# One Wo pair of the weight stream held in free columns of two PSUM banks and copied to the SBUF ring by VectorE

## Chip, cores and metric

The kernel runs on one core of a Trainium2 chip. The metric is the device time of one execution in microseconds (us). Times of a kernel are given as the median of several runs; the profile is of one further execution.

## What is computed

Two branches share the input x (2048 rows of 640 numbers, bfloat16), and a gate mixes them. Branch A is attention with a small memory that is carried from one segment of 32 rows to the next, 64 segments in all; branch B is a gated feed-forward block. Cut to what matters:

```python
g = sigmoid((x * gate_w).sum(-1, keepdims=True))
for s in range(64):                          # branch A, in order: mem feeds the next segment
    h = concat([mem, xs], axis=1)            # 8 memory rows + 32 rows of x
    q, k, v = h @ Wq, h @ Wk, h @ Wv         # 32 heads of 192
    p = softmax(where(mask, q @ k.T * scale, -1e9))
    o = (p @ v) @ Wo                         # 32*192 -> 640
    mem, out_s = o[:, :8], o[:, 8:]
b = (gelu(x @ w_gate) * (x @ w_up)) @ w_down # branch B
return g * a + (1 - g) * b
```

The memory makes the 64 segments a strict chain: segment s + 1 cannot form Q, K and V before segment s has its output.

## The kernel before

**Three stages.** The kernel first computes branch B and the gates and stores B in HBM. A second stage ("left") forms Q and K for the last 8 rows of x of every segment at once, since these do not depend on the memory; it runs over four octets of heads, uses all eight PSUM banks in turn, and stores the result in HBM. Then come the 64 segments, which take most of the time.

**One segment.** The heads are worked on in four octets. `PROG` (from line 491) is the order of the work inside a segment, written out by hand as a list of steps: ("q", o), ("k", o) and ("v", o) multiply the 32 rows by the weights of octet o (L997 for Q and K, L1025 for V, five pieces of 128 rows of the weight each); ("tq", o) and ("tk", o) transpose the result (L1009); ("sc", o) are the scores (L1071, L1082), ("sm", o) the softmax, ("pt", o) and ("pte", o) the transposed probabilities and their copy to SBUF; ("pv", o) is probabilities times V (L1148, L1150) with the copies out of PSUM by ScalarE (L1158) and VectorE ("uT lo" L1162, "uT hi" L1164). ("wo", o, i) multiplies by two pairs of Wo: `wo_part` takes the 24 pairs in order, four matmuls each (L1177), accumulating in PSUM bank 7. A segment ends with the seam: the result is copied out by VectorE (L1239) and ScalarE (L1241), transposed (L1251 to L1256), and ScalarE writes the new memory rows (L1261), for which the next segment's first Q matmul waits. Vl matmuls (L1036), which prepare V of the left rows for one octet per segment, stand in the seam: up to three pieces ahead of the transposes and the rest behind them.

**The PSUM banks.** Banks 0 to 3 rotate for Q, K, V and the transposes, bank 4 is for Vl, banks 5 and 6 for the scores of even and odd octets and for the transposed probabilities, bank 7 for the Wo sum. A bank has 2 KB per partition. The scores take the first 640 bytes of banks 5 and 6 (4 times 40 float32), the transposed probabilities stay inside those.

**Resident and streamed weights.** The weights of branch A are cut into 84 pieces: 60 of Q, K and V (3,072 bytes per partition, 384 KB) and 24 pairs of Wo (2,560 bytes per partition, 320 KB), 245,760 bytes per partition in all. They do not fit into the 200,128 bytes that SBUF has for them. So a planner, which runs when the kernel is built (from line 541), picks the fewest pieces to stream such that the others fit beside a ring of at least `MINRING` = 18,432 bytes; it picks them at equal steps of estimated time along the segment. The others stay in SBUF from their first load on. The build has 23 streamed pieces, 14 of Q, K and V (q0.3, q1.0, k1.0, k1.3, q2.1, k2.1, k2.3, q3.1, k3.2, v0.0, v0.1, v1.1, v2.1, v3.0, named by octet and piece) and 9 pairs of Wo (1, 2, 5, 9, 11, 14, 17, 21, 23), and a ring of 20,416 bytes.

**The ring.** `ring_load` (L578) takes the next bytes of the ring and has SyncE (SP) issue the load; it wraps at the end. A load waits until the matmuls that read the ring bytes before it are done, so some six or seven pieces are in the ring at once, each at some point between issue and use. SP issues all loads of a segment in one order, the order of use, mixed with the loads of the left rows ("stg", L898), of x, and of branch B's rows, and the stores of the output. `issue_ring` and `piece` (from L587) issue a streamed piece at the latest when the program that is being written out comes to its use; on the chip SP runs ahead of TensorE by as much as the ring allows.

**Waits.** Each tile is a region of SBUF or PSUM (a PSUM bank is one region), and `_Sched` works out from reads and writes what each operation waits for. The engines run their own streams in order.

Of the kernel before, what the change touches and what calls it, by code (L numbers as in the profile page):

```python
# [221 lines left out]
def _build(nc, A_x, A_mem0, A_Wq, A_Wk, A_Wv, A_Wo, seg_len, w_gate, w_up, w_down,  # L222
# [136 lines left out]
    def sreg(o, nbytes, plo=0, phi=128):  # L359
        return Rg("sb", o, o + nbytes, plo, phi)  # L360
# [123 lines left out]
    def piece_size(key):  # L484
        return GO if key[0] == 3 else GQ

    def piece_view(key, o):
        if key[0] == 3:
# [10 lines left out]
    assert NOCT == 4  # L499
    WOP = 6  # L500
    COST = dict(q=0.168, k=0.168, v=0.18, sc=0.6, pt=0.2, pv=0.42, wo=0.285, tq=0.15, tk=0.3)
# [23 lines left out]
    tseg = tt + 0.6  # L525
    npieces = len(order)
    assert npieces == len(set(order)) == 3 * KT * NOCT + NCH // 2
    tot_bytes = sum(piece_size(k) for k in order)
    nstream = 0
    while True:  # L530
        streamed = set()
        for k in range(nstream):
            target = (k + 0.5) * tseg / nstream
            best = min((i for i in range(npieces) if i not in streamed
                        and (order[i][0] == 3 or order[i][2] < (KT - 1 if order[i][0] < 2 else 2))), key=lambda i: abs(tcons[i] - target))
            streamed.add(best)
        if tot_bytes - sum(piece_size(order[i]) for i in streamed) <= res_space - MINRING:
            break
        nstream += 1
    resident_list = [i for i in range(npieces) if i not in streamed]  # L540
    stream_list = [i for i in range(npieces) if i in streamed]
    ring_bytes = res_space - (tot_bytes - sum(piece_size(order[i]) for i in streamed))
    assert ring_bytes <= ffn_base
# [28 lines left out]
    ring_ptr = [0]  # L572
    NSEM = ring_bytes // GO + 2

    def ring_load(key, name):
        n = piece_size(key)
        if ring_ptr[0] + n > ring_bytes:
            ring_ptr[0] = 0  # L578
        o = ring_ptr[0]
        ring_ptr[0] += n  # L580
        reg = sreg(o, n)
        S_.add("sp", lambda e: e.dma_start(piece_view(key, o), piece_src(key)), writes=[reg],
               dma_sem="ring%d" % (stream_counter[0] % NSEM), name=name)
        stream_counter[0] += 1
        return piece_view(key, o), reg
# [3 lines left out]
    def issue_ring(seg, upto):  # L589
        done = issued.get(seg, 0)  # L590
        while done <= upto:
            key = order[stream_list[done]]
            ring_of[(seg, key)] = ring_load(key, "ring s%d p%d" % (seg, done))
            done += 1
        issued[seg] = done

    def piece(seg, key):
        oi = order_index[key]
        assert oi == last_req.get(seg, -1) + 1, "pieces must be consumed in `order`"
        last_req[seg] = oi  # L600
        if seg == 0:
            load_late(oi + LATE)
        if key in res_off:
            assert slot_class[key] != 1 or key in late_in
            return piece_view(key, res_off[key]), r_res[key]
        issue_ring(seg, stream_pos[key])
        return ring_of[(seg, key)]

    late = [key for key in order if slot_class.get(key) == 1]
    late_in = set()  # L610
# [291 lines left out]
    def left_store(o_, s0, s1):  # L902
        st = lst[o_ % 2]
        for lo in range(s0, s1, NSEG // 4):
            hi = lo + NSEG // 4
            S_.add("pool" if o_ == NOCT - 1 else "sp", lambda e, lo=lo, hi=hi: e.dma_start(
                qkl[lo:hi].rearrange("s p c -> p s c")[:, :, 2 * LW * o_:2 * LW * (o_ + 1)],
                st[:, lo:hi].rearrange("p s m c -> p s (m c)")),
                reads=[sreg(ffn_base + o_ % 2 * STB + STB // NSEG * s0, STB // NSEG * (s1 - s0))],
                writes=[Rg("qk", 64 * o_ + lo, 64 * o_ + hi)], dma_sem="lst%d_%d" % (o_ % 2 if o_ < NOCT - 1 else 2, 4 * lo // NSEG),  # L910
                name="left store")

    def first_loads():
        stg_load(0, 0)
        issue_ring(0, 4)

    OB = 7
    nbk = [0]
    for o_ in range(NOCT):
        st, rst_ = lst[o_ % 2], r_lst[o_ % 2]  # L920
        nh = 2 if o_ == NOCT - 1 else 1
        gs2 = [[left_piece((m, o_, k)) for k in range(KT)] for m in range(2)]
        if o_ == NOCT - 1:
            load_late_within(ffn_base, ffn_base + STB)
        for h in range(nh):
            n0, n1, s0, s1 = h * NL // nh, (h + 1) * NL // nh, h * NSEG // nh, (h + 1) * NSEG // nh
            for m in range(2):
                gs = gs2[m]
                for i in range(12):
                    bk = nbk[0] % 8  # L930
                    nbk[0] += 1
                    c = i if m == 0 else kslot(i)
                    S_.add("pe", [lambda e, k=k, g_=gs[k][0], i=i, bk=bk, n0=n0, n1=n1: e.matmul(  # L933
                        ps[:, bk, 0:n1 - n0], g_[:, i * 128:(i + 1) * 128], XL[:, k, n0:n1], start=(k == 0), stop=(k == KT - 1))
                        for k in range(KT)], reads=[x[1] for x in gs] + [r_XL], writes=[r_ps[bk]],
                        name="left o%d m%d c%d" % (o_, m, i))
                    dst = st[:, s0:s1, m, c * M:(c + 1) * M]
                    src = ps[:, bk, 0:n1 - n0].rearrange("p (s i) -> p s i", i=M)
                    rgh = [sreg(ffn_base + o_ % 2 * STB + STB // nh * h, STB // nh)]
                    if i % 2:  # L940
                        S_.add("act", lambda e, dst=dst, src=src: e.activation(out=dst, in_=src, func=ACTF.Copy),
                               reads=[r_ps[bk]], writes=rgh, name="left evac")
                    else:
                        S_.add("dve", lambda e, dst=dst, src=src: e.tensor_copy(out=dst, in_=src),
                               reads=[r_ps[bk]], writes=rgh, name="left evac")
            if h + 1 < nh:
                left_store(o_, s0, s1)
        if o_ == 0:
            mem_init()
            b_load(0)  # L950
            hl_load(4)
            S_.add("dve", lambda e: e.memset(ps[:, OB, :], 0.0), writes=[r_ps[OB]])
        if o_ + 1 < NOCT:
            issue_left(sum(key[1] <= o_ + 1 for key in left_stream) - 1)
        else:
            first_loads()
        left_store(o_, s0, s1)

    S_.add("pool", lambda e: e.memset(pl_sb, 0.0), writes=[r_p])
    S_.add("pool", lambda e: e.memset(Ks[64:128, 8:12, :], 0.0), writes=[r_Kz[0]])  # L960
    S_.add("pool", lambda e: e.memset(Ks[0:64, 12:16, :], 0.0), writes=[r_Kz[1]])
# [64 lines left out]
            ps[32 * j:32 * j + 32, bk, 0:384], lhs, g_[:, 384 * j:384 * (j + 1)],  # L1026
            start=(k == 0), stop=(k == KT - 1), tile_position=(0, 32 * j)) for j in range(4)]

    VB = 4
    vl_left = {}  # L1030

    def vl_mms(s, o, k, g_, rg_):
# [151 lines left out]
    def segment(s):  # L1184
        g, q = s // 4, s % 4
        for item in PROG:
            kind, i = item[0], item[1] if len(item) > 1 else None
            if kind in ("q", "k"):
                m = "qk".index(kind)
                bank = misc_bank()  # L1190
                cmode(s, m, i, bank)
                rows_evac(m, bank)
            elif kind == "stga":
                if s > 0:
                    stg_load(s, 0)
                left_fill(s, 0)
            elif kind == "stgb":
                stg_load(s, 1)
            elif kind == "ost":
                if s > 0:  # L1200
                    out_store(s - 1)
            elif kind == "bld":
                if s > 0:
                    b_load(s)
            elif kind == "hld":
                if s + 1 < NSEG:
                    h_load(s + 1)
            elif kind == "hll":
                if 0 < s < NSEG - 5:
                    hl_load(s + 5)  # L1210
            elif kind == "put":
                if 0 < s < NSEG - 4:
                    hl_put(s + 4)
            elif kind == "mix":
                if s > 0:
                    mix_rows(s - 1)
            elif kind == "tq":
                row_transp(s, 0, i)
            elif kind == "tk":
                row_transp(s, 1, i)  # L1220
            elif kind == "sm":
                probs(s, i)
            elif kind == "sc":
                scores(s, i)
            elif kind == "v":
                v_oct(s, i)
            elif kind == "pt":
                p_transp(s, i)
                if i == 0:
                    p_evac(s, i)  # L1230
            elif kind == "pte":
                p_evac(s, i)
            elif kind == "pv":
                pv_oct(s, i)
            else:
                wo_part(s, item)
# [112 lines left out]
```

## Time and profile before

| | |
|---|---|
| median of 3 runs | 2014.24 us (2010.03 to 2020.6) |
| profiled execution | 2022.26 us, its span in the profile 2020.4 us |
| segments 1 to 62 in the profile | 331.7 to 1991.6 us |

The page of the profile gives busy time, share of the span and number of instructions per engine (PE is TensorE's matmuls, PEld its weight loads, DVE VectorE, ACT ScalarE, POOL GpSimd), then tenths of busy time in 40 equal slices, the DMA queues, and the chain of work that ended last. "Idle before" a group of instructions is named by what ended it. A row of the waits reads: engine and line, what it waited for, us in total, times, longest. A timeline row reads: start, duration, engine, line, operation, how many, and in brackets the idle time before it.

### The profile page before, as it was taken

Reading aid. Unit: us, or ns where it says so; the run is one execution under the profiler, and the core shown is the slowest. Engines: PE = TensorE matmul, PEld = TensorE weight load, DVE = VectorE, ACT = ScalarE, POOL = GpSimd, SP = SyncE. Lnnn points to the kernel's source line nnn. Section 1 sums busy time; section 2 is a strip of 40 time slices with the busy share of each in tenths; the row PEclk is TensorE's granted clock in tenths of the full one; section 3 lists DMA queues with packets and bytes.
Section 4 is the critical chain, followed back from the end, with each engine's and each line's share of the span. In section 5 each row is a group of like instructions: output and inputs, shape, how many; then the busy total and the mean of one; then the engine's idle time right before and its main releaser. Section 6 shows DMA issues by size and latency. Waiting matters only on the chain.

```text
span 2020.4 us, 77475 instructions
## 1 busy us (share of the span) xinstructions
PE 1934.8 (96%) x32897; PEld 1139.4 (56%) x32923; DVE 984.1 (49%) x3215; ACT 846.3 (42%) x2308; POOL 270.8 (13%) x1123
## 2 busy tenths in 40 slices
PE   8999978999999999999999999999999999999999
PEld 4544455555555555555555555555555555555555
DVE  2222324555555555555555555555545555555555
ACT  2222233444444444444444444444444444444444
POOL 2000010111111111111111111111111111111111
PEclk9999989999999999999999999999999999999999
DMA  9706699999999999999999999999999999999998
GB/s 303 213 27 72 183 294 328 332 339 326 327 339 334 323 328 333 335 337 336 340 333 336 331 322 309 335 328 328 330 327 333 327 319 338 336 331 325 330 333 296
DMA packets 399670, 621.18 MB, mean 307 GB/s; under 512 B 91348, under 2 KB 276700, under 8 KB 399324
## 3 DMA queue, kind: packets, MB, share of 16 engines
q1 hardware_dynamic: 387500, 607.82, 90.0%
q10 hardware_dynamic: 10992, 5.27, 1.0%
q8 instruction: 257, 4.21, 0.8%
q0 software_dynamic: 832, 3.15, 0.5%
q14 instruction: 89, 0.73, 0.1%
HBM read 594.99 MB, written 21.11 MB: 305 GB/s over the span
## 4 chain that ended last, share of the span: by engine, by line
PE 76%; DMA 17%; SPq 2%; issue 2%; ACT 2%; POOL 1%; DVE 1%; ACTq 0%; POOLq 0%
PE ps L1177 20%; PE ps L997 18%; DMA arena<-in_A_Wv_dram 9%; PE ps L1025 9%; DMA arena<-in_A_Wo_dram 5%; PE ps L1009 4%; PE ps L933 4%; PE ps L1148 4%; PE ps L834 3%; PE ps L831 3%; PE ps L1082 2%; PE ps L849 2%; PE ps L1036 2%; PE ps L1071 2%; PE ps L1150 1%
## 5 line engine op out<-in xcount | busy, mean ns | idle before, releaser
L997 PE MATMUL ps<-arena 128*32 128x384 bf16 x10240 | 493.5, 328 | 20.0 <-DMA arena<-in_A_Wq_dram 12.1
L1177 PE MATMUL ps<-arena 128*40 128x320 bf16 x6144 | 471.2, 301 | 9.3 <-DMA arena<-in_A_Wo_dram 8.5
L1177 PEld LDWEIGHTS ps<-arena 128*40 128x40 bf16 x6144 | 294.1, 100 | 161.5 <-issue 51.9
L997 PEld LDWEIGHTS ps<-arena 128*32 128x32 bf16 x10240 | 239.7, 96 | 166.3 <-ACT arena L1261 14.1
L1003 ACT ACTIVATE arena<-ps 128x384 bf16<-128x384 f32 x512 | 250.9, 490 | 175.4 <-PE ps L997 170.4
L1025 PE MATMUL ps<-arena 128*32 128x384 bf16 x5120 | 280.3, 329 | 24.1 <-DMA arena<-in_A_Wv_dram 23.3
L964 POOL COPY arena<-arena 128x96 bf16<-128x96 bf16 x256 | 67.2, 263 | 1401.7 <-PE ps L997 325.0
L1158 ACT ACTIVATE arena<-ps 128x320 bf16<-128x320 f32 x256 | 111.6, 436 | 265.4 <-PE ps L1150 265.4
L1060 ACT ACTIVATE arena<-ps 128x384 bf16<-128x384 f32 x256 | 125.5, 490 | 173.4 <-PE ps L1025 172.1
L1025 PEld LDWEIGHTS ps<-arena 128*32 128x32 bf16 x5120 | 125.6, 96 | 124.6 <-DMA arena<-in_A_Wv_dram 50.1
L1093 DVE TENSOR_REDUCE arena<-ps 104x4 f32<-104x160 f32 x256 | 83.2, 325 | 210.7 <-PE ps L1082 210.7
L968 POOL COPY arena<-arena 64x32 bf16<-64x32 bf16 (+1 forms) x768 | 165.3, 215 | 47.3
L1162 DVE CAST arena<-ps 64x160 bf16<-64x160 f32 x256 | 80.4, 314 | 182.1 <-PE ps L1150 181.5
L1009 PE MATMUL ps<-arena 128*128 128x128 bf16 x1536 | 165.6, 222 | 0.7 <-issue 0.7
L1013 DVE COPY arena<-ps 128x384 bf16<-128x384 bf16 x256 | 89.6, 350 | 120.4 <-PE ps L1009 120.4
L1020 ACT ACTIVATE arena<-ps 64x128 bf16<-64x128 bf16 x512 | 137.1, 268 | 6.2
L1009 PEld LDWEIGHTS ps<-arena 128*128 128x128 bf16 x1536 | 87.5, 97 | 75.9 <-issue 21.5
L1148 PE MATMUL ps<-arena 128*128 128x160 bf16 (+1 forms) x768 | 129.0, 258 | 0.0
L1131 DVE TENSOR_TENSOR arena<-ps,arena 128x320 bf16<-128x320 bf16 x256 | 125.3, 489 | 6.0
L1150 PE MATMUL ps<-arena 128*128 128x64 bf16 (+1 forms) x768 | 123.5, 201 | 0.0
L1107 DVE TENSOR_REDUCE arena<-ps 104x4 f32<-104x160 f32 x256 | 81.9, 320 | 62.6 <-ACT ps L1105 59.8
L1105 ACT ACTIVATE ps<-ps 104x160 f32<-104x160 f32 x256 | 72.1, 282 | 94.6 <-DVE ps L1095 93.0
(91 smaller groups left out, 2095.3 us busy)
## 6 DMA issues: line engine op xcount, KB each, us to landing
arena<-in_A_Wo_dram SPq DMA_DIRECT2D x591, 320.0 KB, 5.6
arena<-in_A_Wk_dram SPq DMA_DIRECT2D x336, 384.0 KB, 5.0
arena<-in_A_Wv_dram SPq DMA_DIRECT2D x332, 384.0 KB, 5.7
arena<-in_A_Wq_dram SPq DMA_DIRECT2D x272, 384.0 KB, 5.3
arena<-left_qk_scratch SPq DMA_DIRECT2D x128, 96.0 KB, 5.0
left_qk_scratch<-arena SPq DMA_DIRECT2D x12, 768.0 KB, 8.5
left_qk_scratch<-arena POOLq DMA_DIRECT2D x4, 768.0 KB, 9.3
arena<-in_A_x_dram SPq DMA_DIRECT2D x4, 640.0 KB, 8.7
```

What stands on the lines that cost most here:

```text
L968: S_.add("pool", lambda e, a=a, b=b, lo=lo, hi=hi, sa=sa: e.tensor_copy(out=Ks[lo:hi, a:b, L:R], in_=stg[o // 2][lo:hi, o % 2, 1, sa:sa + ...
L997: S_.add("pe", [lambda e, j=j, k=k, g_=g_: e.matmul(ps[32 * j:32 * j + 32, bank, 0:384], Hb[hb][:, k, 0:L], g_[:, 384 * j:384 * (j + 1)], ...
L1003: S_.add("act", lambda e: e.activation(out=rows_sb[m], in_=ps[:, bank, 0:384], func=ACTF.Copy), reads=[r_ps[bank]], writes=[r_rows[m]], na ...
L1009: S_.add("pe", [lambda e, c=c: e.transpose(pv[:, c * 128:(c + 1) * 128], rows_sb[m][:, c * 128:(c + 1) * 128], ident) for c in range(3)], ...
L1020: S_.add("act", lambda e, a=a, lo=lo: e.activation(out=Ks[lo:lo + 64, a:a + 4, 0:L], in_=src[lo:lo + 64, 1], func=ACTF.Copy), reads=[r_ps[ ...
L1025: return [lambda e, j=j: e.matmul(ps[32 * j:32 * j + 32, bk, 0:384], lhs, g_[:, 384 * j:384 * (j + 1)], start=(k == 0), stop=(k == KT - 1) ...
L1060: S_.add("act", lambda e: e.activation(out=v_sb[o % NVB], in_=ps[:, bank, 0:384], func=ACTF.Copy), reads=[r_ps[bank]], writes=[r_v[o % NVB ...
L1131: S_.add("dve", lambda e: e.tensor_tensor(out=PTm, in0=apx(pv[:, 0:104], [[64, 2], [0, 4], [1, R]]), in1=apx(mbd, [[0, 2], [1, 4], [0, R]] ...
L1148: return [lambda e: e.matmul(full, v[:, e0:e0 + 128], PTm[:, ia:ib], start=True, stop=False, skip_group_check=True), lambda e: e.matmul(pa ...
L1150: lambda e: e.matmul(part, vl[:, e0:e0 + 128], apx(PTl[:, ia, 0, 0:1], [[16, 4 * n], [M, 2], [1, M]]), start=False, stop=True, skip_group_ ...
L1158: S_.add("act", lambda e: e.activation(out=apx(u[:, 0, 0, :], [[2 * R, 2], [3 * R, 4], [1, R]]), in_=ps[:, A, 0:2 * W].rearrange("p (c t r ...
L1177: fns.append(lambda e, g_=g_, i=i, c=c, j=j, tl=tl, cc=cc, u=u: e.matmul(ps[64 * j:64 * j + R, OB, 0:DH], u[:, tl, cc, :], g_[:, i, DH * j ...
```

## The change

Wo pair 20, the first pair of step ("wo", 3, 1), becomes a "hosted" piece: neither resident nor streamed from HBM. It lies for the whole of the 64 segments in columns of PSUM banks 5 and 6 that scores and probabilities do not use (bytes 640 to 1,920 of each). In every segment two new steps, ("cp", 0) after ("pv", 3) and ("cp", 1) after ("wo", 2, 1), have VectorE copy its two halves, 128 partitions by 640 bfloat16 each, into a slot of the ring, where the matmuls of pair 20 read it. The order of all the other steps stays.

The planner leaves pair 20 out of the bytes to be placed, and picks anew. The changed build has 22 streamed pieces: 13 of Q, K and V (q0.3, q1.0, k1.0, k1.3, q2.3, k2.2, q3.0, q3.3, k3.3, v0.0, v1.0, v2.0, v3.0) and 9 pairs of Wo (0, 2, 4, 8, 10, 13, 16, 21, 23), and a ring of 19,904 bytes, through which pair 20 passes as a 23rd slot without a load.

Once, in the left stage, pair 20 is loaded into the ring, transposed by TensorE (ten 128x128 blocks), copied to SBUF by VectorE, and after the stage transposed back by TensorE into banks 5 and 6. The first loads of segment 0 ahead of it are four instead of five.

```diff
-            ("pv", 3), ("wo", 2, 1), ("bld",), ("wo", 2, 2), ("wo", 3, 0), ("wo", 3, 1), ("wo", 3, 2)]
+            ("pv", 3), ("cp", 0), ("wo", 2, 1), ("cp", 1), ("bld",), ("wo", 2, 2), ("wo", 3, 0), ("wo", 3, 1),
+            ("wo", 3, 2)]
...
+    HC = 2 * 4 * R
+    HOSTS = {20: [(5, HC, 0, Dm), (6, HC, Dm, Dm)]}
+    hosted = [(3, p) for p in HOSTS]
...
+    tot_bytes = sum(piece_size(k) for k in order if k not in hosted)
...
+    def host_copy(s, n):
+        p, (bank, col, c0, ncol) = copies[n]
+        key = (3, p)
+        if (s, key) not in ring_of:
+            issue_ring(s, sum(j < order_index[key] for j in stream_list) - 1)
+            o, reg = ring_slot(key)
+            ring_of[(s, key)] = piece_view(key, o), reg
+            ring_live.append((o, o + GO, (s, key)))
+        o = ring_of[(s, key)][1].lo + 2 * c0
+        S_.add("dve", lambda e: e.tensor_copy(out=bview(o, 2 * ncol), in_=psb(bank)[:, col:col + ncol]),
+               reads=[r_ps[bank]], writes=[sreg(o, 2 * ncol)], name="host%d s%d" % (n, s))
...
-        issue_ring(0, 4)
+        issue_ring(0, 3)
...
+    def host_turn():
+        for n, p in enumerate(HOSTS):
+            hv, rh = host_src[p]
+            for i in range(2):
+                bk = nbk[0] % 8
+                nbk[0] += 1
+                o = HT + n * GO + 2 * Dm * i
+                S_.add("pe", [lambda e, c=c, i=i, bk=bk, hv=hv: e.transpose(
+                    psb(bk)[:, c * 128:c * 128 + 128], hv[:, i, c * 128:c * 128 + 128], ident)
+                    for c in range(KT)], reads=[rh, r_ident], writes=[r_ps[bk]], name="hostT")
+                S_.add("dve", lambda e, bk=bk, o=o: e.tensor_copy(out=bview(o, 2 * Dm), in_=psb(bk)[:, 0:Dm]),
+                       reads=[r_ps[bk]], writes=[sreg(o, 2 * Dm)], name="hostT evac")
+
+    def host_fill():
+        for n, p in enumerate(HOSTS):
+            for bank, col, c0, ncol in HOSTS[p]:
+                o = HT + n * GO + 2 * c0
+                S_.add("pe", [lambda e, c=c, bank=bank, col=col, o=o: e.transpose(
+                    psb(bank)[:, col + c:col + c + 128], bview(o + 2 * c, 256), ident)
+                    for c in range(0, ncol, 128)], reads=[sreg(o, 2 * ncol), r_ident], writes=[r_ps[bank]], name="hostT2")
...
+        if o_ == 1:
+            host_load()
+        if o_ == 2:
+            host_turn()
...
+    host_fill()
...
+            elif kind == "cp":
+                host_copy(s, i)
```

More of the change, by code (lines that the diff above doesn't have):

```diff
@@ L527, in _build @@
     assert npieces == len(set(order)) == 3 * KT * NOCT + NCH // 2
-    tot_bytes = sum(piece_size(k) for k in order)
+    HC = 2 * 4 * R
+    assert HC + Dm <= 1024
+    VB = 4
+    HOSTS = {20: [(5, HC, 0, Dm), (6, HC, Dm, Dm)]}
+    hosted = [(3, p) for p in HOSTS]
+    hosted_i = [order.index(k) for k in hosted]
+    copies = [(p, x) for p in HOSTS for x in HOSTS[p]]
+    tot_bytes = sum(piece_size(k) for k in order if k not in hosted)
     nstream = 0
@@ L533, in _build @@
             target = (k + 0.5) * tseg / nstream
-            best = min((i for i in range(npieces) if i not in streamed
+            best = min((i for i in range(npieces) if i not in streamed and i not in hosted_i
                         and (order[i][0] == 3 or order[i][2] < (KT - 1 if order[i][0] < 2 else 2))), key=lambda i: abs(tcons[i] - target))
@@ L539, in _build @@
         nstream += 1
-    resident_list = [i for i in range(npieces) if i not in streamed]
+    resident_list = [i for i in range(npieces) if i not in streamed and i not in hosted_i]
     stream_list = [i for i in range(npieces) if i in streamed]
@@ L573, in _build, with ring_slot @@
     NSEM = ring_bytes // GO + 2
-    def ring_load(key, name):
+    ring_live = []
+    def ring_slot(key):
         n = piece_size(key)
@@ L580, in ring_load @@
         ring_ptr[0] += n
-        reg = sreg(o, n)
+        assert all(b <= o or o + n <= a for a, b, _ in ring_live)
+        return o, sreg(o, n)
+    def ring_load(key, name):
+        o, reg = ring_slot(key)
         S_.add("sp", lambda e: e.dma_start(piece_view(key, o), piece_src(key)), writes=[reg],
@@ L593, in issue_ring @@
             ring_of[(seg, key)] = ring_load(key, "ring s%d p%d" % (seg, done))
+            ring_live.append((ring_of[(seg, key)][1].lo, ring_of[(seg, key)][1].hi, (seg, key)))
             done += 1
@@ L605, in piece @@
             return piece_view(key, res_off[key]), r_res[key]
-        issue_ring(seg, stream_pos[key])
+        if key not in hosted:
+            issue_ring(seg, stream_pos[key])
+        ring_live[:] = [x for x in ring_live if x[2] != (seg, key)]
         return ring_of[(seg, key)]
+    def host_copy(s, n):
[3 more added lines that the diff above has]
+            issue_ring(s, sum(j < order_index[key] for j in stream_list) - 1)
+            o, reg = ring_slot(key)
+            ring_of[(s, key)] = piece_view(key, o), reg
[3 more added lines that the diff above has]
+               reads=[r_ps[bank]], writes=[sreg(o, 2 * ncol)], name="host%d s%d" % (n, s))
     late = [key for key in order if slot_class.get(key) == 1]
@@ L914, in first_loads, with host_load @@
         stg_load(0, 0)
-        issue_ring(0, 4)
+        issue_ring(0, 3)
     OB = 7
     nbk = [0]
+    host_src = {}
+    HT = wsB_off["Q"]
+    assert len(HOSTS) * GO <= wsB_off["PTm"] - HT
+    def host_load():
+        for p in HOSTS:
+            host_src[p] = ring_load((3, p), "host init")
+    def host_turn():
[17 more added lines that the diff above has]
+                    for c in range(0, ncol, 128)], reads=[sreg(o, 2 * ncol), r_ident], writes=[r_ps[bank]], name="hostT2")
     for o_ in range(NOCT):
@@ L1027, in v_mms @@
             start=(k == 0), stop=(k == KT - 1), tile_position=(0, 32 * j)) for j in range(4)]
-    VB = 4
     vl_left = {}
```

## Prediction

> **What bounds the kernel now.** First the page: busy time, DMA queues, the chain that ended last.
>
> ```profile
> span 2020.4 us, 77475 instructions
> ...
> PE 1934.8 (96%) x32897; PEld 1139.4 (56%) x32923; DVE 984.1 (49%) x3215; ACT 846.3 (42%) x2308; POOL 270.8 (13%) x1123
> ...
> q1 hardware_dynamic: 387500, 607.82, 90.0%
> ...
> PE 76%; DMA 17%; SPq 2%; issue 2%; ACT 2%; POOL 1%; DVE 1%; ACTq 0%; POOLq 0%
> ```
>
> TensorE looks like the bound, yet one DMA queue is busy for 90% of the span and 17% of the last chain is transfers. VectorE, which gets new work, is busy for half. So the two candidates have to be compared over the segments alone. The window view has one row for them; the rows of L1261, the end of a segment's seam, give its first and last one.
>
> ```profile
> L1261 ACT ACTIVATE arena<-ps 128x40 bf16<-128x40 f32 x63 | 12.8, 203 | 27.9 <-PE ps L1256 27.9
> ...
> L1261 ACT ACTIVATE arena<-ps x2: 203/204/204, 331.7 to 357.8; 128x40 bf16<-128x40 f32 x2
> ...
> L1261 ACT ACTIVATE arena<-ps x2: 203/203/203, 1966.0 to 1991.6; 128x40 bf16<-128x40 f32 x2
> ...
> 331.70:1991.60 1659.90, 1605.86 (x30260) 963.28 (x30256) 873.12 (x2976) 745.53 (x2108) 238.07 (x1051) 1.00 0.97 331
> ```
>
> 63 ends have 62 segments between them: 1659.9 / 62 = 26.77 us each. The last two columns are the DMA share, 0.97, and 331 GB/s. One segment therefore moves 331 x 26.77 = 8.86 MB, and a queue that was never idle would move 331 / 0.97 = 341 GB/s and need 26.0 us for it. The transfers nearly fill the segment.
>
> How much TensorE loses to that is read from the waits in the same window. The weight loader (PEld) waits for the weights' DMA too, since it stands ahead of the matmul; its waits are the fuller measure, because the idle time of PE hides behind the modelled ends of the matmuls before.
>
> ```profile
> PEld ps L1025 <- DMA arena<-in_A_Wv_dram: 45.2, 86, 2.3
> ...
> PE ps L1025 <- DMA arena<-in_A_Wv_dram: 20.3, 38, 1.9
> ...
> PEld ps L1177 <- DMA arena<-in_A_Wo_dram: 17.0, 36, 2.1
> ...
> PE ps L1177 <- DMA arena<-in_A_Wo_dram: 5.9, 11, 1.8
> ...
> PE ps L997 <- ACT arena L1261: 5.1, 15, 0.4
> ...
> PEld ps L997 <- DMA arena<-in_A_Wk_dram: 3.0, 7, 0.7
> ```
>
> 45.2 + 17.0 + 3.0 = 65.2 us, or 1.05 us per segment. Without them TensorE's own pace would be 26.77 - 1.05 = 25.7 us, and the DMA's need of 26.0 us is above that: the weight stream is the bound, by a little, and TensorE comes next at once. The chain and the timeline show such a wait in V:
>
> ```profile
> 1516.66 0.68 PE ps L997 x13
> 1517.34 6.12 DMA arena<-in_A_Wv_dram
> 1523.46 0.04 issue
> 1523.50 0.83 PE ps L1025 x16
> ```
> ```profile
> 1521.36 1.16 PE L1025 MATMUL ps<-arena 128*32 128x384 bf16 x24
> 1523.50 0.83 PE L1025 MATMUL ps<-arena 128*32 128x384 bf16 x16 [0.98 <-DMA arena<-in_A_Wv_dram]
> ```
>
> A Q matmul ends, its ring slot goes to a V piece, and 6.12 us later that lands 0.98 us late. The 24 matmuls ahead are six pieces in 1.16 us; two of them, v0.0 and v0.1, are streamed neighbours, followed by the late v1.1. A piece of 393 kB takes 393 / 341 = 1.15 us of the queue, so these neighbours cannot both come in time.
>
> **The change part by part.** The profiled execution took 2022.3 us, 8.0 more than the median; the sum is made against it and then shifted.
>
> *The stream.* Both plans have nine Wo pairs; the changed one has one V piece less, 384 KB = 0.393 MB of 8.86. The DMA then needs 8.47 / 0.341 = 24.8 us, 0.9 below TensorE's 25.7. The V piece that goes is v0.1, one of the two neighbours above. So TensorE becomes the bound; what remains are waits where the loads come unevenly. Bounds: all of the 65 us goes, or none (then the depth of the ring was the cause, third rival). I take four fifths, -52 us, nearer to the upper end because the gap of 0.9 us is as large as the waits of today; a fifth is left for uneven loads.
>
> *The copies.* Two copies of 128x640 bfloat16 from PSUM per segment are new on VectorE. The grouped rows by shape bracket them:
>
> ```profile
> L1013 DVE COPY arena<-ps 128x384 bf16<-128x384 bf16 x256 | 89.6, 350 | 120.4 <-PE ps L1009 120.4
> ...
> L944 DVE CAST arena<-ps 128x512 bf16<-128x512 f32 x36 | 24.9, 692 | 50.2 <-PE ps L933 45.5 <-ACT arena L941 4.7
> ...
> L944 DVE CAST arena<-ps 128x256 bf16<-128x256 f32 x24 | 10.2, 425 | 16.3 <-PE ps L933 16.3
> ...
> L815 DVE COPY arena<-ps 128x1024 bf16<-128x1024 bf16 x4 | 2.8, 692 | 6.7 <-PE ps L802 3.4 <-PE ps L799 3.3
> L815 DVE COPY arena<-ps 128x512 bf16<-128x512 bf16 x4 | 1.7, 414 | 0.0
> ```
>
> L815 is the same kind, bfloat16 in PSUM to SBUF: (692 - 414) / 512 = 0.54 ns an element, so 414 + 128 x 0.54 = 0.48 us for 640. From float32 (L944) an element costs 1.04 ns and 640 would take 692 + 128 x 1.04 = 0.83 us; that is the other end. I take 0.48, the row of the same types.
>
> The Trainium skill, "VectorE: DVE Perf Modes", section "Rules for kernel authors", speaks against this: on a matmul's output one accepts the 1x rate of a PSUM source. At that page's 0.96 GHz this is 1.04 ns an element. This trace's L815 rows, at 0.54, are twice as fast; still it is the second rival.
>
> Do the copies end in time? The tail of one segment:
>
> ```profile
> 1532.81 2.90 PE L1177 MATMUL ps<-arena 128*40 128x320 bf16 x40
> 1532.92 0.32 DVE L1162 CAST arena<-ps 64x160 bf16<-64x160 f32 x1 [1.29 <-PE ps L1150]
> 1533.27 0.33 DVE L1164 CAST arena<-ps 64x160 bf16<-64x160 f32 x1
> ...
> 1535.75 0.29 DVE L1239 CAST arena<-ps 128x128 bf16<-128x128 f32 x1 [2.16 <-PE ps L1177]
> ```
>
> The 40 matmuls are pairs 14 to 23; 24 precede pair 20, which is due at 1532.81 + 24 x 2.90 / 40 = 1534.55. VectorE is free at 1533.60 and starts a row 0.03 us after the one before, so the copies end at 1534.11 and 1534.62; with the 0.04 us of "issue" in the chain above pair 20 starts at 1534.66, 0.1 us late. Over 64 segments that is +6 us (end to end: 0, if a pair ahead waits for its own load anyway, to +49 at 0.83 us a copy, 0.77 us late each). Behind the waiting pair stand pairs 21 to 23 and the seam, so all of it counts. L1239, next on VectorE, starts at 1535.75, 1.1 us behind the copies, and is not held up. The copies' own waits, for bank 5 or 6 and for a ring slot that pair 2 and q3.3 left some 7 us earlier, end long before; the next scores write these banks several us into the next segment.
>
> *The seam.* The V piece that is no longer streamed is one of octet 0. Vl of octet 0, one segment in four, now has a fourth resident piece, which stands behind the seam's transposes and covers the wait for L1261: the 15 waits of 5.1 us above. I take -4; the work itself only moves.
>
> *Left stage and start.* Ten transposes, at 0.09 us each by the row below, are added to a stage in which TensorE is the bound: +1. The ten after it, and the fill's wait for the last evictions, lie in TensorE's wait of 11.16 us at the start of segment 0, which ends with a load. One 384 KB piece fewer is placed ahead of that load and pair 20 is fetched earlier: -1. Should that wait be gone, the ten transposes would cost +1.
>
> ```profile
> 1512.19 0.27 PE ps L1009 x3
> ```
> ```profile
> 290.94 2.43 PE L997 MATMUL ps<-arena 128*32 128x384 bf16 x28 [11.16 <-DMA arena<-in_A_Wq_dram]
> ```
>
> *Sum.* -52 + 6 - 4 + 1 - 1 = -50: 1972.3 on the profiled execution's scale, 1964 on the median's.
>
> **Rivals.**
>
> *Half of the waits stay*: other neighbours (q3.0, q3.3, k3.3) come late instead. For it: all of Q and K in octet 3 is now streamed closer together; against it: Q and K hardly wait today (3.0 us). -33 + 6 - 4 = -31: 1983.
>
> *The copies run at the slow rate.* Each at 0.83 us: +49 instead of +6, so -7: 2007. Against it stand the L815 rows, for it only that none of them is 640 wide at a column offset.
>
> *The ring's depth is the bound, and the kernel becomes slower.* Pair 20 takes a place in the ring and carries no load, and the ring has 512 bytes less. SP often waits for a place:
>
> ```profile
> SPq L201 <- PE ps L997: 250.6, 282, 1.7
> SPq L201 <- PE ps L1177: 163.9, 197, 2.5
> ```
>
> If a load's time does not fall with the bytes in the queue, V waits as today, and the loads that reach back across pair 20's place (pairs 21 and 23 and the first of the next segment) start one place, about 1.15 us, later. It decides from a landing of about 6.6 us on (six places of 26.77 / 23 us, less 0.4 to issue). With two of them late by 0.3 us, 0.6 x 62 = +37, with the copies and the seam +39: 2053. Against it: a share of 0.97 says that the queue is full, and landings have medians of 5.0 to 5.7 us:
>
> ```profile
> arena<-in_A_Wo_dram SPq DMA_DIRECT2D x591, 320.0 KB, 5.6
> arena<-in_A_Wk_dram SPq DMA_DIRECT2D x336, 384.0 KB, 5.0
> arena<-in_A_Wv_dram SPq DMA_DIRECT2D x332, 384.0 KB, 5.7
> ```
>
> The Trainium skill, "DMA: Bandwidth & Descriptors", section "Where 436 GB/s comes from", puts the ceiling of the ports at 435 GB/s: by that 8.86 MB would need 20.4 us, the queue would have room, and the waits would be this rival's. The trace's 341 GB/s at full share does not bear that out.
>
> *It does not do what it says*: excluded as far as the build goes, which has 22 loads per segment instead of 23.
>
> **How the numbers follow.** About 0.5% (10 us) is what a measurement of this kernel can tell from no change. Forecast 0.60: 1964, with 1942 (all waits gone, copies free: -65 - 4 = -69 or 1945, a little less for the pace of the first segment) to 1975. Half of the waits 0.20: 1975 to 2000. Slow copies 0.09: about 2007, so "same" 0.05, faster 0.02, slower 0.02. Depth 0.08: slower. Nothing measurable 0.03. Faster 0.82, same 0.08, slower 0.10. The range 1942 to 2007 leaves out the depth case and the far ends, under 2 in 10.
>
> **What would show it.** In the changed profile: a segment near 25.9 us; DMA share at or below 0.97 with about 327 GB/s; V's waits for DMA down from 45 us to about 10; copies of 0.48 us, 128 of them; PE waits for VectorE at L1177 of about 0.1 us per segment; the 15 waits of L997 for L1261 gone. The forecast is wrong if the DMA waits only move to other lines, if landings stay over 6 us, or if the copies take 0.8 us.

## The result, and the profile after

The changed kernel takes 1993.4 us (median of 4 runs, 1992.4 to 1995.6) against 2014.1 us: a ratio of 0.9885, 95% interval 0.9857 to 0.9912, so 1.15% faster. The prediction was 1964 us, 2.5% faster, with 1942 to 2007 as its range: the sign and the range hold, but less than half of the forecast gain came. The profiled executions lie further apart than the medians (spans 2020.4 and 1990.7 us), since that of before was 8 us above its median.

The page of the changed kernel, the lines that answer to those of before:

```profile
span 1990.7 us, 77519 instructions
...
PE 1930.8 (97%) x32917; PEld 1137.5 (57%) x32943; DVE 1041.4 (52%) x3345; ACT 846.0 (42%) x2308; POOL 270.7 (14%) x1123
...
q1 hardware_dynamic: 378428, 583.04, 88.7%
...
PE 86%; DMA 7%; ACT 1%; POOL 1%; issue 1%; DVE 1%; SPq 1%; ACTq 0%; POOLq 0%
```

24.8 MB less went over the queue, VectorE has 57 us more work, and transfers hold 7% of the last chain where they held 17%. Line numbers shift: L997 is now L1060 (Q, K), L1025 is L1088 (V), L1177 is L1239 (Wo), L1261 is L1325; the copies are L635. The window of segments 1 to 62, with the ends of the seam that bound it, and the waits inside it:

```profile
L1325 ACT ACTIVATE arena<-ps x63: 203/203/204, 330.2 to 1962.2; 128x40 bf16<-128x40 f32 x63
...
330.20:1962.20 1632.00, 1600.41 (x30259) 959.42 (x30259) 927.81 (x3100) 745.25 (x2109) 238.06 (x1051) 1.00 0.96 322
```
```profile
PEld ps L1239 <- DVE arena L635: 17.3, 62, 0.3
...
PEld ps L1088 <- DMA arena<-in_A_Wv_dram: 10.7, 21, 2.4
...
PEld ps L1239 <- DMA arena<-in_A_Wo_dram: 5.5, 14, 1.0
...
PE ps L1088 <- DMA arena<-in_A_Wv_dram: 4.7, 7, 2.0
...
PEld ps L1060 <- DMA arena<-in_A_Wk_dram: 2.2, 7, 0.5
PE ps L1144 <- POOL arena L1031: 2.2, 6, 0.8
...
PEld ps L1088 <- DMA arena<-in_A_Wo_dram: 1.9, 4, 1.0
...
PE ps L1133 <- POOL arena L1031: 1.4, 2, 0.9
...
PE ps L1239 <- DMA arena<-in_A_Wo_dram: 1.2, 2, 0.7
```

A segment takes 1632.0 / 62 = 26.32 us, 0.45 less than the 26.77 of before, or 27.9 us over the window (the profiled executions lie 9 us further apart than the medians). But the weight loader's waits for weights fell from 65.2 to 10.7 + 5.5 + 2.2 + 1.9 = 20.3 us: by 45 of the 52 that were forecast, V's to the 10 us named in the forecast. So most of the waits went and the time did not follow by as much. Either the rows over-counted what the waits cost (theory A), or they were right and other waits took the time back (rival B): the copies, and GpSimd's copies of the left rows (L1031), for which the scores now wait at times.

The tail of a segment shows the copies:

```profile
1431.04 3.03 PE L1239 MATMUL ps<-arena 128*40 128x320 bf16 x40
...
1431.50 0.33 DVE L1226 CAST arena<-ps 64x160 bf16<-64x160 f32 x1
1431.86 0.89 DVE L635 COPY arena<-ps 128x640 bf16<-128x640 bf16 x2
1432.80 0.94 PEld L1239 LDWEIGHTS ps<-arena 128*40 128x40 bf16 x16 [0.28 <-DVE arena L635]
...
1434.11 0.29 DVE L1303 CAST arena<-ps 128x128 bf16<-128x128 f32 x1 [1.37 <-PE ps L1239]
```
```profile
L635 DVE COPY arena<-ps 128x640 bf16<-128x640 bf16 x128 | 56.9, 486 | 2.0
```

A copy takes 486 ns, and the 40 matmuls around pair 20 take 3.03 us instead of 2.90: 0.13 us, where 0.1 was forecast. Nothing later on VectorE is held up (L1303 waits for TensorE).

### The profile page after: what moved, and what is told of

It reads as the page before. It is cut to its first block, busy times and chain, and to the rows that moved or that the text cites. A ratio compares the mean times of both kernels' runs of the same rounds, so it can differ in the third digit from the quotient of the medians.

```text
span 1990.7 us, 77519 instructions
## 1 busy us (share of the span) xinstructions
PE 1930.8 (97%) x32917; PEld 1137.5 (57%) x32943; DVE 1041.4 (52%) x3345; ACT 846.0 (42%) x2308; POOL 270.7 (14%) x1123
## 4 chain that ended last, share of the span: by engine, by line
PE 86%; DMA 7%; ACT 1%; POOL 1%; issue 1%; DVE 1%; SPq 1%; ACTq 0%; POOLq 0%
PE ps L1239 23%; PE ps L1060 21%; PE ps L1088 10%; PE ps L1072 6%; PE ps L1210 4%; PE ps L991 4%; DMA arena<-in_A_Wv_dram 3%; PE ps L1144 3%; PE ps L863 3%; PE ps L860 3%; PE ps L1133 2%; DMA arena<-in_A_Wo_dram 2%; PE ps L878 2%; PE ps L1098 2%; PE ps L1212 1%
## 5 line engine op out<-in xcount | busy, mean ns | idle before, releaser
L1060 PE MATMUL ps<-arena 128*32 128x384 bf16 x10240 | 494.8, 329 | 12.4 <-DMA arena<-in_A_Wq_dram 8.7
L1239 PE MATMUL ps<-arena 128*40 128x320 bf16 x6144 | 474.5, 301 | 1.5 <-DMA arena<-in_A_Wo_dram 1.2
L1239 PEld LDWEIGHTS ps<-arena 128*40 128x40 bf16 x6144 | 290.4, 100 | 160.1 <-issue 48.7
L1060 PEld LDWEIGHTS ps<-arena 128*32 128x32 bf16 x10240 | 239.8, 96 | 161.1 <-ACT arena L1325 12.5
L1088 PE MATMUL ps<-arena 128*32 128x384 bf16 x5120 | 266.0, 328 | 9.1 <-DMA arena<-in_A_Wv_dram 7.8
L1088 PEld LDWEIGHTS ps<-arena 128*32 128x32 bf16 x5120 | 127.5, 96 | 93.2 <-DMA arena<-in_A_Wv_dram 14.4
L1031 POOL COPY arena<-arena 64x32 bf16<-64x32 bf16 (+1 forms) x768 | 165.4, 215 | 47.3
L1224 DVE CAST arena<-ps 64x160 bf16<-64x160 f32 x256 | 80.4, 314 | 150.9 <-PE ps L1212 149.9
```

Source lines behind the costliest of these rows:

```text
L1031: S_.add("pool", lambda e, a=a, b=b, lo=lo, hi=hi, sa=sa: e.tensor_copy(out=Ks[lo:hi, a:b, L:R], in_=stg[o // 2][lo:hi, o % 2, 1, sa:sa + ...
L1060: S_.add("pe", [lambda e, j=j, k=k, g_=g_: e.matmul(ps[32 * j:32 * j + 32, bank, 0:384], Hb[hb][:, k, 0:L], g_[:, 384 * j:384 * (j + 1)], ...
L1088: return [lambda e, j=j: e.matmul(ps[32 * j:32 * j + 32, bk, 0:384], lhs, g_[:, 384 * j:384 * (j + 1)], start=(k == 0), stop=(k == KT - 1) ...
L1239: fns.append(lambda e, g_=g_, i=i, c=c, j=j, tl=tl, cc=cc, u=u: e.matmul(ps[64 * j:64 * j + R, OB, 0:DH], u[:, tl, cc, :], g_[:, i, DH * j ...
```

## The experiments

Each ran against the kernel before on the same chip. Ratios are to that kernel, with the 95% interval.

**What the stream costs in all, before.** In `ring_load`:

```diff
+        dst, src = piece_view(key, o), piece_src(key)
+        if name.startswith("ring s") and int(name[6:].split()[0]) >= 2:
+            dst, src = (dst[:, 0:1, 0:320], src[:, 0:1, 0:320]) if key[0] == 3 else (dst[:, 0:384], src[:, 0:384])
-        S_.add("sp", lambda e: e.dma_start(piece_view(key, o), piece_src(key)), writes=[reg],
+        S_.add("sp", lambda e: e.dma_start(dst, src), writes=[reg],
```

> The kernel before, with every streamed load of segments 2 to 63 cut to the first quarter of its columns (the rest of the slot keeps older weights, so three quarters of the stream are left out); order, waits and ring unchanged. It takes away what the weight stream costs. Theory A (the loss to the loads was over-counted: the weight loader's 65 us of waits partly lie beside matmuls still running, and the true loss is about 36 us of the median): 1978 us. Rival B (all 65 us were lost to the loads, and what the change saved was eaten by new waits): 1949 us.

1976.6 us; ratio 0.980 (0.9776 to 0.9824), or -40 us of 2014. In its profile (segments from 332 to 1950 us) the loads have no part any more:

```profile
332.00:1950.00 1618.00, 1593.66 (x30337) 970.63 (x30326) 874.58 (x2979) 748.52 (x2115) 240.67 (x1055) 1.00 0.38 100
```
```profile
PEld ps L1028 <- DMA arena<-in_A_Wv_dram: 0.9, 2, 0.5
```

The share is 0.38 and V's 45 us of waits are 0.9. Theory A holds: the loss was 40 us (35 to 45 by the interval), not 65. The weight loader's wait begins while the matmuls before it still run, so a part of its 129 waits cost nothing. The trace of before shows it in single waits: at 1523.50 us the loader had waited 1.37 us and the matmuls 0.98, and at 1549.01 us the loader had waited 0.23 us for a V load inside a row of 40 V matmuls that run on without a gap:

```profile
1548.02 1.83 PE L1025 MATMUL ps<-arena 128*32 128x384 bf16 x40
```

The idle time of PE for the loads of V and Wo, 20.3 + 5.9 = 26.2 us in the rows of before, erred the other way. The truth lay between. A second reason for the gap is not excluded: once the loads are gone, the loader waits longer for ScalarE's copy of V out of PSUM (L1060, here L1063), 18.8 us instead of 6.9. What that costs was not measured. First before, then with quarter loads:

```profile
PEld ps L1025 <- ACT arena L1060: 4.0, 19, 0.4
...
PEld ps L1148 <- ACT arena L1060: 2.9, 9, 0.4
```
```profile
PEld ps L1151 <- ACT arena L1063: 10.1, 31, 0.4
...
PEld ps L1028 <- ACT arena L1063: 8.7, 31, 0.4
```

**What is left of it after the change.** The same edit in the changed kernel.

> The changed kernel with the same cut of its streamed loads. What is left of the loss to loads goes. Theory A: little is left, about 10 us of 1993, so 1983 us, and 5 to 7 us over the kernel before with the same cut, the price of the two copies. Rival B: the 20.6 us of the weight loader's waits for loads all go, 1973 us, and the new waits stand as 24 us over the kernel before with the same cut.

1979.2 us; 0.9813 (0.9789 to 0.9837). The changed kernel without its stream would be 0.9885 - 0.9813 = 0.7% or 14.5 us faster, give or take 7 by the two intervals. And against the kernel before with the same cut it loses 0.9813 - 0.980 = 0.13%, 2.6 us: copies less seam. This is small, but the runs of the two kernels, taken together, hardly overlap (1974.8 to 1977.9 and 1977.8 to 1980.3). That is A's picture; B's 24 us of new waits are not there.

**The copies, moved.** Both go where VectorE was idle:

```diff
-("pte", 3), ("wo", 2, 0), ("pv", 3), ("cp", 0), ("wo", 2, 1), ("cp", 1), ("bld",)
+("pte", 3), ("cp", 0), ("cp", 1), ("wo", 2, 0), ("pv", 3), ("wo", 2, 1), ("bld",)
```

> The changed kernel with both copies moved ahead of step (wo, 2, 0), behind the third octet's probabilities, where VectorE is idle for 1.29 us in the trace of before. Pair 20 then finds its slot filled. Theory A: the 0.115 us per segment that pair 20 starts later in the changed profile goes, -7 us: 1986 us. Rival B (the copies cost more than their wait, by what they displace): -16 us or more, 1977 us; if the copies now delay the copy-out of octet 3's PV result, no gain, 1993 us or more.

1982.7 us; 0.9834 (0.9808 to 0.986), 0.5% or 10 us below the changed kernel's ratio, though the two intervals just overlap and the runs were not taken together. The trace shows where 8 of them are (0.13 us in each of 62 segments): the 40 matmuls are back at 2.90 us, and the copy-out of octet 3 (L1224) starts as soon as before.

```profile
1423.48 0.88 DVE L635 COPY arena<-ps 128x640 bf16<-128x640 bf16 x2
...
1424.90 2.90 PE L1239 MATMUL ps<-arena 128*40 128x320 bf16 x40
1425.01 0.32 DVE L1224 CAST arena<-ps 64x160 bf16<-64x160 f32 x1 [0.65 <-PE ps L1212]
```

**The plan without the hosting.** The `cp` steps go, `HOSTS` is empty, and the streamed set is fixed:

```diff
+    names = "q03 q10 k10 k13 q23 k22 q30 q33 k33 v00 v10 v20 v30".split()
+    keys = [("qkv".index(n[0]), int(n[1]), int(n[2])) for n in names] + [(3, p) for p in (0, 2, 4, 8, 10, 13, 16, 20, 21, 23)]
+    streamed = set(order.index(k) for k in keys)
```

> The changed kernel's choice of streamed pieces and its ring of 19,904 bytes, but pair 20 streamed from HBM as a 23rd load; no copies, nothing in PSUM. A segment's stream is then 8.39 MB, against 8.45 before and 8.06 in the changed kernel. If the gain comes from the fewer bytes: 0.8% fewer bytes, about 2008 us. If it comes from where the loads stand (v0.0 and v0.1 no longer neighbours): the V waits go as in the changed kernel and the copies' 7 us as well, about 1988 us.

2010.1 us; 0.9957 (0.994 to 0.9973). Neither number: the time is near that of "fewer bytes", but the mechanism is not. V's waits do go; Wo's grow, since pairs 20, 21 and 23 are now loads due within four pairs, the last of them 12 matmuls behind the first, 0.9 us at the 2.90 / 40 us of a matmul above:

```profile
PEld ps L1242 <- DMA arena<-in_A_Wo_dram: 29.2, 56, 1.9
...
PEld ps L1091 <- DMA arena<-in_A_Wv_dram: 4.3, 8, 2.2
```

**One load less, in V.** The kernel before; from segment 2 on, in `ring_load`:

```diff
+        if name.startswith("ring s") and int(name[6:].split()[0]) >= 2 and key == (2, 0, 1):
+            dst, src = dst[:, 0:96], src[:, 0:96]
```

> The kernel before, in which from segment 2 on the load of v0.1 brings 96 of its 1,536 columns (the rest of that piece is left out and older weights stand in its place); 22 full loads per segment as in the changed kernel, no copies, nothing hosted. It is the change's saving without its price. If fewer bytes are the cause: -28 us or a ratio near 0.986, a little better than the changed kernel's 0.9885. If the copies cost nothing and something else in the change brought the gain, no change.

1998.2 us; 0.990 (0.9881 to 0.9919): 20 us gained, not 28. It is the saving without copies, yet it gains no more than the whole change, which also parts the other loads and covers the seam. V's waits fall as in the changed kernel:

```profile
PEld ps L1028 <- DMA arena<-in_A_Wv_dram: 9.4, 21, 0.8
```

**One load less, elsewhere.** The same with `key == (0, 2, 1)`.

> The same cut on q2.1, which has no streamed neighbour in V: the same bytes less, at another place, with v0.0 and v0.1 still neighbours. If the bytes alone count, the same ratio as with v0.1 cut, about 0.986; if it counts that the neighbours in V are parted, clearly less gain, 0.993 or more.

2018.0 us against 2018.3; 0.9998 (0.9981 to 1.0015). Nothing. The same bytes are gone, and V waits as ever:

```profile
PEld ps L1028 <- DMA arena<-in_A_Wv_dram: 45.4, 81, 2.9
...
332.00:1950.00 1618.00, 1568.60 (x29638) 943.70 (x29639) 856.65 (x2921) 732.24 (x2069) 236.08 (x1035) 1.00 0.96 319
```

With 319 GB/s instead of 331 the DMA engines still show a share of 0.96. So here the share was no measure of how much the queue could still carry, and the sum of a segment's bytes did not set its time.

**The same bytes, parted.** The kernel before, with one piece exchanged in the plan:

```diff
+    streamed = (streamed - {order.index((2, 0, 1))}) | {order.index((1, 0, 2))}
```

> The kernel before with one change in the choice of streamed pieces: k0.2, early in the segment, is streamed instead of v0.1. 23 loads and 8.45 MB per segment as before, the same ring, nothing hosted. If the sum of the bytes bounds the kernel: ratio 1.00. If it is the crowd of loads that come due together in V, as the runs with v0.1 and q2.1 cut suggest: V's waits fall to a fifth, and the ratio is near 0.99, less what the added load costs at the start of the segment, where a load put ahead of the others made Q and K wait.

2016.7 us against 2014.6; 1.0009 (0.9991 to 1.0028). No gain, against my expectation. The ratio is the 1.00 that went with a bound by the sum of the bytes, but the run with q2.1 speaks against that cause, and so do the rows: V's waits go as they should, and turn up in K and at the scores:

```profile
PEld ps L998 <- DMA arena<-in_A_Wk_dram: 38.6, 57, 1.6
...
PEld ps L1072 <- POOL arena L969: 9.5, 14, 1.8
...
PEld ps L1026 <- DMA arena<-in_A_Wv_dram: 5.4, 13, 1.1
```

A load less at another place (q2.1) gains nothing, and parting the crowd at the same number of loads gains nothing here and 0.4% in the plan alone. A load less in the crowd gains 1%. In the two plans tried with 23 loads the crowd only changes its place.

**The left rows' load, earlier.** The copies early, and:

```diff
-("q", 1), ("tk", 0), ("k", 1), ("stga",), ("sc", 0)
+("stga",), ("q", 1), ("tk", 0), ("k", 1), ("sc", 0)
```

> The changed kernel with early copies (ratio 0.983 to before), and the load of the first left rows issued three steps earlier. In the changed profile that issue stands on SyncE's queue behind a ring load that waits for pair 20, 0.8 us later than before, and TensorE then waits at the scores for the copies of GpSimd that need it. If that is a price of the change: -3 to -4 us, ratio near 0.981; if those waits are covered, the same as the early copies alone.

2009.7 us; 0.9954 (0.9936 to 0.9973): 1.2% worse than the early copies alone. SyncE's queue shows why. First this kernel, then that with the early copies alone:

```profile
SPq L201 <- PE ps L1060: 234.2, 281, 1.9
SPq L927 <- PE ps L1239: 186.4, 57, 3.4
```
```profile
SPq L201 <- PE ps L1060: 214.2, 251, 1.4
SPq L201 <- PE ps L1239: 176.6, 189, 2.8
```

The load of the left rows (L927) needs the tile that the Wo matmuls up to pair 17 read. Issued earlier, it stands on SyncE for 186.4 / 57 = 3.3 us a segment, and the ring loads behind it stand with it. K then waits, where with the early copies alone its row had 3.7 us:

```profile
PEld ps L1060 <- DMA arena<-in_A_Wk_dram: 44.2, 82, 1.8
PEld ps L1060 <- DMA arena<-in_A_Wq_dram: 18.2, 30, 1.8
```

So the few us of waits at the scores in the changed kernel cannot be had back this way.

**The put, earlier.** The copies early, and ("put",) moved from behind ("sm", 2) to ahead of ("sc", 2).

> The changed kernel with early copies, and GpSimd's copy of the new left rows of x (step put) moved ahead of the third octet's scores. In the profiles of before and after TensorE waits for it in every fourth segment, 15 times 0.65 us. If that wait is exposed: -8 to -10 us, ratio near 0.979. If another wait takes its place in the V phase: about 0.983.

1979.7 us; 0.980 (0.9779 to 0.9821), the fastest of the kernels that load all their weights, 2% under the kernel before and some 0.8% under the changed one. In the changed kernel every fourth segment waits for GpSimd here; the row is gone with the move:

```profile
PE ps L1098 <- POOL arena L787: 9.8, 15, 0.7
```

About 7 of those 9.8 us came back; the interval overlaps that of the early copies (0.9834), so this size is not certain.

## Why the prediction was right in sign and wrong in size

- *The waits for loads, "65.2 us, or 1.05 us per segment"*: this is the step that failed, and with it the stream's term, -52. The waits were taken at their full length as lost time. Measured by taking the loads away the loss is 40 us (the run with quarter loads). The loader's rows overstate by 25 us, 20 to 30 by the interval; so TensorE's own pace is not 25.7 us a segment but, by the ends of the seam in that run, (1945.0 - 330.4) / 62 = 26.04:

```profile
L1264 ACT ACTIVATE arena<-ps x63: 204/204/205, 330.4 to 1945.0; 128x40 bf16<-128x40 f32 x63
```

- *"The weight stream is the bound, by a little"*: not in the sense used. 26.0 us came from dividing the rate by the share 0.97. Cutting q2.1 took 4.4% of the bytes and no time.
- *"I take four fifths, -52 us"*: of the 40 us, 40 - 14.5 = 26 went, 64%. The term was 26 (give or take 9 by the three intervals), not 52. Four fifths of 40 would have been 32: of the 26 us that were missing, 20 lie in the base and 6 in the fraction.
- *The copies, +6*: 486 ns each (0.48 forecast), 0.13 us a segment in the tail shown, 8 us; moving them gained about 10 us by the ratios. Right. At the float32 rate of the L944 rows it would have been 0.83 us. The 1x rate that the Trainium skill's "VectorE: DVE Perf Modes" has for a PSUM source ("Rules for kernel authors") is that rate; the measurement of 486 ns decides against it for this bfloat16 copy.
- *The seam, -4*: the 15 waits of L997 for L1261, 5.1 us in all, have no counterpart after. With the copies' 7 to 8 us this makes the 2.6 us between the two kernels with quarter loads. Right.
- *The start*: segment 0 ends at 330.2 instead of 331.7 us; about right in sum. The load that its first matmul waits for came 5.7 us earlier (285.26 instead of 290.94), more than the 1 us forecast; 4.2 us of that were lost again within segment 0, 2.5 of them in a second wait for a Q load (0.9 us before, 3.4 after):

```profile
285.26 2.43 PE L1060 MATMUL ps<-arena 128*32 128x384 bf16 x28 [5.34 <-DMA arena<-in_A_Wq_dram]
```

- *The sum with the measured terms*: -26 + 2.6 = -23, or 1991. It closes because 26 was worked out from the same ratios, and so it is no check; the medians gave -20.7.
- *The rivals*: "half of the waits stay" is the nearest, and for a reason it did not name. Slow copies and the depth of the ring did not come: landings fell (Wv 5.7 to 5.3 us by the page) and V's waits with them.

```profile
arena<-in_A_Wv_dram SPq DMA_DIRECT2D x269, 384.0 KB, 5.3
```

- *Missed*: SyncE's order. The left rows' load stands behind a K load, which in the changed kernel waits for a Wo matmul, by its time pair 20's. One segment of before and one of after, in the timeline:

```profile
1507.45 0.43 SPq L898 DMA_DIRECT2D arena<-left_qk_scratch  x1
...
1510.12 0.20 ACT L1261 ACTIVATE arena<-ps 128x40 bf16<-128x40 f32 x1 [0.41 <-PE ps L1256]
```
```profile
1460.45 0.43 SPq L927 DMA_DIRECT2D arena<-left_qk_scratch  x1
...
1462.03 0.20 ACT L1325 ACTIVATE arena<-ps 128x40 bf16<-128x40 f32 x1 [0.47 <-PE ps L1320]
```

It is issued 1.6 us ahead of the seam's end instead of 2.7 (medians over the segments: 1.6 and 2.4), and the scores' 2.2 + 1.4 us of waits for L1031 above are probably its price. Its share in the 14.5 us that remain was not measured alone, and stays open.

## What to carry to other kernels

The waits of the weight loader were too high a measure of what TensorE lost to its loads (65 us for 40), and the idle time of the matmul rows too low (26); the cost itself is found by cutting the loads to a quarter with the order kept, one run. This stream, nearly balanced with the compute, was not bounded by its sum of bytes. So ask which loads come due together, and take one out there: in the one other place that was tried it brought nothing, and moved it crowded another place. A load on a shared issue queue should not be moved ahead of others when it waits for something that is free later than what they need; here that cost 1.2%.

## What the runs showed of the hardware

- The DMA share stayed at 0.96 to 0.97 while the rate fell from 331 to 319 GB/s, with one load in 23 cut. As far as these rows show, a share near one is not a queue that can carry no more. With loads of a quarter it was 0.38, and those landed in 2.0 us where whole pieces take 5.0 to 5.7:

```profile
arena<-in_A_Wv_dram SPq DMA_DIRECT2D x310, 96.0 KB, 2.0
```

- A VectorE copy of 640 bfloat16 from PSUM at a column offset of 640 bytes took 486 ns. The L815 rows, 414 ns for 512 and 692 ns for 1024, give 483 for that length: the offset cost nothing that shows.
